# Spreading the weight conversions over all twelve attention tiles, with earlier loads and the conditional copies on another queue

## The chip, the cores and the metric

One core of a Trainium2 chip runs the whole kernel. The metric is the device time of one execution in microseconds. Several executions are compared by their median.

## The reference

Three layers run one after the other on a tensor of 2 batches, 768 positions and 384 = 8 x 48 features.

```python
# 1. linear attention with decay, per batch b and head h
cur = einsum('bhd,bhe->bhde', u * k_t, v_t)
y_t = einsum('bhd,bhde->bhe', r_t, state + cur)
state = w * state + einsum('bhd,bhe->bhde', k_t, v_t)
# 2. mixing over tokens, then over channels
h = relu(x.T @ w_tok1) @ w_tok2;  u = x + h.T
x = u + relu(u @ w_ch1) @ w_ch2
# 3. one expert per token (8 experts); the choice can be carried over from the token before
out = p[e] * (relu(x @ w1[e]) @ w2[e])
```

The weights of layer 2 (`w_tok1`, `w_tok2`, `w_ch1`, `w_ch2`) are 64-bit floats in memory. The kernel needs each of them as two 32-bit numbers, a high and a low part, so that three fast matmuls give a product of nearly full precision. Making these two parts is the conversion that this document is about.

## The kernel before

**Attention.** The 12 tiles (`NT`) are 128 positions each, six per batch. The loop `for t in range(NT)` works on several tiles at once: in pass t, TensorE makes the scores of tile t+1 and the values of tile t, VectorE multiplies r and k of tile t+2 with decay powers (`pre_rk`), masks the scores of t+1 (`masks`), forms a product of t+2 (`pre_beta`) and adds up x of tile t (`finish`). ScalarE copies `ks` (`pre_ks`), scales the state (`state`), makes the bonus of tile t+1 in eight small steps (`pre_bonus2`, written `bon`), and casts x to its high part `xh`; GpSimd subtracts to get the low part `xl`. Behind `finish`, `turn` transposes x of the tile before, `mix1` adds the first token matmul, and from tile 7 on `mix2` does a piece of the second one for batch 0; its VectorE step adds into `xT`. In tile 10 `usplit` splits the first part of `xT` (ScalarE `uh`, VectorE `ul`).

**Conversions.** There are 16 blocks (`conv`), two for each of eight weight tiles. Block n goes through these steps:

- a load of 768 KB into one of two `raw` buffers (`conv_load`, SyncE's queue);
- abs(n): ScalarE takes the magnitude of the upper words (`conv_abs`, L305);
- part A: two VectorE steps (L314, L315); part B: one (L319); part C: one (L321), after which the next raw block is loaded into the freed buffer. `conv_do(k)` runs the next k parts;
- hi(n) and lo(n): ScalarE casts the result to the high part (L281), GpSimd subtracts for the low part (L282). This is `conv_finish`, called at the beginning of the next part A or by itself.

Blocks 0 to 7 belong to the attention loop, blocks 8 and 9 to the stretch behind it (`conv_tail`), and blocks 10 to 15 to the first twelve channel steps (`later`). Before the change, `CONV_T` lists the eight tiles that hold a block: in each of them `conv_abs` stands ahead of `values`, parts A and B ahead of `finish`, part C behind it:

```python
        if t in CONV_T:
            conv_abs(CONV_T.index(t))
        values(t)
...
        if t in CONV_T:
            conv_do(CONV_N[t])
        else:
            conv_finish()
        finish(t)
        if t in CONV_T:
            conv_do(3 - CONV_N[t])
```

**What sets the order.** The order on each engine is the order in which the program is written; each engine takes its instructions strictly one after the other. PSUM tiles come from five buffers in turn, so the score tiles of a later pass wait until `finish` has read an earlier one. SyncE's queue issues all loads and, in `finish`, a copy from `yscr` into x (L477) that is carried out only if a decay lies outside the fast path's range (`bad > 0`); with these inputs it is not. Loads of `rk` have four buffers, those of `v` three.

Of the kernel before, what the change touches and what calls it, by code (L numbers as in the profile page):

```python
# [9 lines left out]
F32 = mybir.dt.float32  # L10
# [10 lines left out]
DM = H * D  # L21
NCH = S // 128
NT = B * NCH
# [5 lines left out]
W_LO, W_HI = 0.55, 1.25  # L29
WARM = (6, 12, 3)  # L30
T1 = 4
CONV_T = (2, 3, 4, 5, 6, 8, 9, 10)
CONV_B = (1, 1, 1, 1, 1, 1, 0, -1, 0, 0)
ABS_NEXT = (10, 11, 12, 13, 14)
ABS_B = (0, 3)
CONV_N = (0, 0, 2, 2, 2, 2, 2, 2, 2, 2, 2, 0)
HI_MIN, HI_MAX = (float(x) for x in np.array([0x38100000, 0x47EFFFFF], np.int32).view(np.float32))

CST = {}
# [38 lines left out]
def _emit(ctx, tc, a_in, wu, u_row, wt1, wt2, wc1, wc2, wgl, wex, cst_in, cst_a, out):  # L78
    nc = tc.nc
# [7 lines left out]
    yscr = dram.tile([NT, 128, DM], F32, name="yscr")  # L87
# [11 lines left out]
    def C(name):  # L99
        a, b = CST[name]  # L100
        return cst[:, a:b]
# [10 lines left out]
    ap = actx.enter_context(tc.tile_pool(name="ap", bufs=2))  # L112
# [21 lines left out]
    def load_a(t, part=None):  # L134
        if t not in a_t:
            rk = ap.tile([128, 1024], F32, tag="rk", name=f"rk{t}", bufs=4)
            v = ap.tile([128, DM], F32, tag="v", name=f"v{t}", bufs=3)
            a_t[t] = (rk, v)
        for p, (dst, c0) in enumerate(zip(a_t[t], (0, 1536))):
            if part is None or p == part:  # L140
                nc.sync.dma_start(out=dst, in_=a_in[t, :, c0:c0 + dst.shape[1]])
# [43 lines left out]
    for k in range(1, 7):  # L185
# [8 lines left out]
        if k == 5:  # L194
            bad = nc.values_load(bad_i[0:1, 0:1], min_val=0, max_val=1)
# [59 lines left out]
    conv = []  # L255
# [3 lines left out]
    conv_raw, conv_pend, cpool_, wb2 = [], [], [], []  # L259
    nload = [0]  # L260

    def conv_load():
        n = nload[0]
        if n >= len(conv) or (n >= 12 and not cpool_):
            return
        nload[0] += 1
        k, h = conv[n]
        src = wt1 if k == 0 else wt2 if k == 1 else None
        if src is None:
            src = (wc1, wc2)[k % 2][(k - 2) // 2]  # L270
        if n < 12:
            raw = rawp.tile([128, 768, 2], I32, tag="raw", name="raw")
        else:
            raw = cpool_[0].tile([128, 768, 2], I32, tag=f"e{n - 12}", name="raw")
        nc.sync.dma_start(out=raw.rearrange("p n t -> p (n t)"), in_=src.bitcast(I32)[:, h * 1536:(h + 1) * 1536])
        conv_raw.append(raw)

    def conv_finish():
        if conv_pend:
            f, hs, ls = conv_pend.pop()  # L280
            nc.scalar.copy(hs, f)  # L281
            nc.gpsimd.tensor_tensor(out=ls, in0=f, in1=hs.bitcast(F32), op=ALU.subtract)  # L282
# [4 lines left out]
    def conv_abs(n):  # L287
        k, h = conv[n]
        name = ("t1", "t2", "c10", "c20", "c11", "c21", "c12", "c22")[k]
        if h == 0:  # L290
            pool = wtp if k < 2 else wbl if k < 5 else wb2[0]
            W[name] = tuple(pool.tile([128, 1536], F32R, tag=f"b{2 * k + j}", name=name) for j in range(2))
        raw = conv_raw.pop(0)
        parts = tuple(x[:, h * 768:(h + 1) * 768] for x in W[name])
        if wb2:
            if n < 12:
                late[n % 2] = cpool_[0].tile([128, 1536], I32, tag=f"raw{6 + n % 2}", name="f")
            f, mag = late[n % 2][:, 0:768], late[n % 2][:, 768:1536].bitcast(F32)
        else:
            if n % 2:  # L300
                f = hp.tile([128, 768], I32, tag="row", name="f", bufs=1)
            else:
                f = ap.tile([128, 768], I32, tag="f", name="f", bufs=1)
            mag = f.bitcast(F32)
        nc.scalar.activation(out=mag, in_=raw[:, :, 1].bitcast(F32), func=ACTF.Abs)  # L305
        conv_mag[n] = raw, mag, f, parts

    def conv_parts():
        for n in range(len(conv)):
            conv_finish()  # L310
            if n not in conv_mag:
                conv_abs(n)
            raw, mag, f, parts = conv_mag.pop(n)
            nc.vector.tensor_scalar(out=mag, in0=mag, scalar1=HI_MIN, scalar2=HI_MAX, op0=ALU.max, op1=ALU.min)  # L314
            nc.vector.tensor_scalar(  # L315
                out=f, in0=mag.bitcast(I32), scalar1=3, scalar2=0x3FFFFFFF, op0=ALU.logical_shift_left, op1=ALU.bitwise_and
            )
            yield
            nc.vector.scalar_tensor_tensor(out=f, in0=raw[:, :, 0], scalar=29, in1=f, op0=ALU.logical_shift_right, op1=ALU.bitwise_or)  # L319
            yield  # L320
            nc.vector.scalar_tensor_tensor(out=f, in0=raw[:, :, 1], scalar=-0x40000000, in1=f, op0=ALU.bitwise_and, op1=ALU.bitwise_or)  # L321
            conv_pend.append((f.bitcast(F32), *parts))
            conv_load()
            if n in ABS_NEXT:
                conv_abs(n + 1)
            yield
        conv_finish()

    tail_at = [-1]

    def conv_tail(n):
        tail_at[0] += 1
        for j in range(2):
            if ABS_B[j] == tail_at[0]:
                conv_abs(8 + j)
        if n < 0:
            conv_finish()
        else:
            conv_do(n)

    conv_work = conv_parts()

    def conv_do(n=3):
        for _ in range(n):
            next(conv_work, None)
# [45 lines left out]
    def scores(t):  # L391
        rk = a_t[t][0]
        at_t[t] = [ps_tile("at0"), ps_tile("at1")]
        for q in range(4):
            for g in range(2):
                r0 = 64 * g
                nc.tensor.matmul(
                    at_t[t][g][:, q * 128:(q + 1) * 128],
                    lhsT=rk[r0:r0 + 64, 512 + q * 128:512 + (q + 1) * 128],
                    rhs=rk[r0:r0 + 64, q * 128:(q + 1) * 128],  # L400
                    start=True,
                    stop=True,
                )
# [29 lines left out]
    def old(t):  # L433
        kp = ps_tile("kp")
        kp_t[t] = kp[:, 0:384].rearrange("p (q e) -> p q e", q=4)
        beta_t[t] = kp[:, 384:392]
        if t % NCH in range(1, NCH - 1):
            nc.tensor.matmul(kp_t[t], lhsT=CA("ident"), rhs=sts[(t - 1) % 3], start=True, stop=False)
# [34 lines left out]
    def finish(t):  # L473
        b, c = divmod(t, NCH)
        x = ap.tile([128, DM], F32, tag="x", name="x")
        nc.vector.tensor_tensor(out=x, in0=y_t.pop(t), in1=bon_t.pop(t).rearrange("p h e -> p (h e)"), op=ALU.add)
        nc.sync.dma_start(out=x, in_=yscr[t], cond=bad > 0, cond_hint=False)  # L477
        xh[t] = ap.tile([128, DM], F32R, tag=f"xh{c}", name=f"xh{t}", bufs=1)
        xl[t] = ap.tile([128, DM], F32R, tag=f"xl{c}", name=f"xl{t}", bufs=1)
        nc.scalar.copy(xh[t], x)  # L480
        nc.gpsimd.tensor_tensor(out=xl[t], in0=x, in1=xh[t].bitcast(F32), op=ALU.subtract)
        xx[t] = x
# [79 lines left out]
    for t in range(NT):  # L562
        if t + 3 < NT:
            load_a(t + 3, 0)
        if t < 2:
            conv_load()
        grow = t + 1 < NT and (t + 1) % NCH < NCH - 1
        if t + 1 < NT:
            old(t + 1)
            scores(t + 1)  # L570
            if t == 0:
                warm_up(WARM[2])
        if t + 2 < NT:
            pre_rk(t + 2)
        if t + 1 < NT:
            masks(t + 1)
            beta(t + 1)
        if t + 2 < NT:
            pre_beta(t + 2)
        if grow:  # L580
            update(t + 1)
            state(t + 1)
        if t in CONV_T:
            conv_abs(CONV_T.index(t))
        values(t)
        if t + 1 < NT:
            pre_bonus2(t + 1)
        if t + 3 < NT:
            load_a(t + 3, 1)
        if t in CONV_T:  # L590
            conv_do(CONV_N[t])
        else:
            conv_finish()
        finish(t)
        if t in CONV_T:
            conv_do(3 - CONV_N[t])
        if t >= 7:
            mix2(*m2.pop(0))
        if t == 10:
            usplit(0)  # L600
        if t >= 1:
            turn(t - 1)
            m1.append(t - 1)
            if t >= T1:
                for _ in range(2):
                    if m1:
                        mix1(m1.pop(0))
        if t + 2 < NT and (t + 2) % NCH < NCH - 1:
            pre_ks(t + 2)
# [649 lines left out]
    with tc.If(nreg > 0):  # L1259
        with tc.tile_pool(name="ov", bufs=1) as ovp:  # L1260
# [9 lines left out]
                out=sel, in0=pfx.unsqueeze(1).to_broadcast([128, NOV, 96]), in1=C("ovn").unsqueeze(2).to_broadcast([128, NOV, 96]), op=ALU.is_equal  # L1270
# [91 lines left out]
```

## Time and profile before

| what | us |
|---|---|
| median of 3 runs | 428.48 (425.42 to 428.80) |
| the profiled execution | 426.03 |
| its span, first to last instruction | 424.5 |
| TensorE busy | 398.8 |
| VectorE busy | 278.4 |
| ScalarE busy | 193.0 |
| GpSimd busy | 90.3 |

A timeline row reads: start in us, duration in us, engine and line, operation, out<-in with the shape, the number of instructions merged into the row, and in brackets how long the engine was idle ahead of it and what released it. The start of a row and the start of the next one tell more than the durations, since one instruction's end overlaps the next one's start by about 0.1 us. DVE is VectorE, ACT is ScalarE, POOL is GpSimd, PE is TensorE and SPq the queue of SyncE.

### The profile page before, as it was taken

To read this page: it belongs to the slowest core of one execution; us is meant where nothing else is said; L and a number is where in the kernel's file an instruction comes from. 1 tells how busy PE (TensorE), PEld (TensorE's weight loads), DVE (VectorE), ACT (ScalarE), POOL (GpSimd) and SP (SyncE) were. 2 spreads that over 40 slices of the span, in tenths; PEclk is the share of its full clock that TensorE was granted. 3 is DMA by queue.
4 is the path that set the end of the run, shared out by engine and by line. 5 is a ranking of instruction groups with operands and counts; after the bars stand their busy time and mean duration, and the time that the engine had idled before them with its cause. 6 is when DMAs were issued, how large, how long until landed. Compare 5 with 4: busy or idle time off the path is not lost. (4 is left out here: it accounts for less than half of the span.)

```text
span 424.5 us, 8637 instructions
## 1 busy us (share of the span) xinstructions
PE 398.8 (94%) x3348; PEld 380.6 (90%) x3348; DVE 278.4 (66%) x592; ACT 193.0 (45%) x459; POOL 90.3 (21%) x83
## 2 busy tenths in 40 slices
PE   6898699997898899999999999999999999999994
PEld 3677688986797899999999999999999999999994
DVE  6869998986989833624361446659677676675431
ACT  1688386783343332112311221642755666654531
POOL 2004345054323310000000001131261132111110
PEclk9998999998999699999999999999999999999998
DMA  7455565333380000100100010881879866663000
GB/s 263 162 174 152 204 218 189 100 90 117 114 350 2 1 2 19 38 0 2 56 2 0 2 56 16 320 312 44 264 287 411 273 216 234 214 203 102 12 30 14
DMA packets 16800, 55.88 MB, mean 132 GB/s; under 512 B 3921, under 2 KB 7795, under 8 KB 16754
## 3 DMA queue, kind: packets, MB, share of 16 engines
q1 hardware_dynamic: 14834, 49.96, 33.7%
q0 software_dynamic: 1920, 5.32, 4.0%
q8 instruction: 27, 0.44, 0.4%
q14 instruction: 19, 0.16, 0.1%
HBM read 52.31 MB, written 5.91 MB: 137 GB/s over the span
## 5 line engine op out<-in xcount | busy, mean ns | idle before, releaser
L1024 DVE TENSOR_TENSOR we<-wr,we 128x768 fp32r<-128x768 f32 x54 | 51.6, 961 | 14.5 <-ACT we L1023 14.2
L353 ACT ACTIVATE hh<-c 128x384 fp32r<-128x384 f32 x48 | 23.5, 490 | 74.7 <-PE c L350 66.1
L354 DVE SCALAR_TENSOR_TENSOR hl<-c,hh 128x384 fp32r<-128x384 f32 x48 | 26.5, 552 | 43.8 <-ACT hh L353 43.8
L353 ACT ACTIVATE hh<-e 128x256 fp32r<-128x256 f32 (+1 forms) x72 | 25.2, 350 | 57.2 <-PE e L350 42.3
L348 PE MATMUL c<-uh,c 128*128 128x384 f32 x144 | 49.2, 342 | 2.1 <-ACT c L281 2.1
L354 DVE SCALAR_TENSOR_TENSOR hl<-e,hh 128x256 fp32r<-128x256 f32 (+1 forms) x72 | 27.2, 378 | 35.2 <-ACT hh L353 35.1
L348 PE MATMUL acc<-hh,c 128*128 128x384 f32 x144 | 50.2, 349 | 0.0
L349 PE MATMUL c<-uh,c 128*128 128x384 f32 x144 | 49.0, 340 | 1.2 <-POOL c L282 1.2
L349 PE MATMUL acc<-hh,c 128*128 128x384 f32 x144 | 48.8, 339 | 0.0
L350 PE MATMUL acc<-hl,c 128*128 128x384 f32 x144 | 48.8, 339 | 0.0
L350 PE MATMUL c<-ul,c 128*128 128x384 f32 x144 | 48.8, 339 | 0.0
L1023 ACT CAST we<-wr 128x768 fp32r<-128x768 f32 x56 | 46.1, 830 | 3.1 <-DMA wr<-in_wex 3.1
L348 PE MATMUL acc<-we,hh 128*128 128x384 f32 x120 | 42.6, 355 | 0.0
L349 PE MATMUL acc<-we,hl 128*128 128x384 f32 x120 | 40.3, 336 | 0.0
L350 PE MATMUL acc<-we,hh 128*128 128x384 f32 x120 | 40.2, 335 | 0.0
L282 POOL TENSOR_TENSOR c<-f,c 128x768 fp32r<-128x768 f32 x12 | 24.3, 2026 | 45.1 <-ACT c L281 45.1
L348 PEld LDWEIGHTS c<-uh,c 128*128 128x128 f32 x144 | 27.7, 192 | 2.4 <-ACT c L281 2.4
L349 PEld LDWEIGHTS c<-uh,c 128*128 128x128 f32 x144 | 27.6, 192 | 1.8 <-POOL c L282 1.8
L349 PEld LDWEIGHTS acc<-hh,c 128*128 128x128 f32 x144 | 27.5, 191 | 0.0
L348 PEld LDWEIGHTS acc<-hh,c 128*128 128x128 f32 x144 | 27.5, 191 | 0.0
L350 PEld LDWEIGHTS acc<-hl,c 128*128 128x128 f32 x144 | 27.5, 191 | 0.0
L350 PEld LDWEIGHTS c<-ul,c 128*128 128x128 f32 x144 | 27.4, 191 | 0.0
(228 smaller groups left out, 945.0 us busy)
## 6 DMA issues: line engine op xcount, KB each, us to landing
wr<-in_wex SPq DMA_DIRECT2D x32, 768.0 KB
raw<-in_wc SPq DMA_DIRECT2D x12, 768.0 KB
rk<-in_a_in SPq DMA_DIRECT2D x12, 512.0 KB
raw<-in_wt SPq DMA_DIRECT2D x4, 768.0 KB
v<-in_a_in SPq DMA_DIRECT2D x12, 192.0 KB
x<-yscr SPq DMA_DIRECT2D x12, 192.0 KB
xs<-rows SPq DMA_DIRECT2D x8, 192.0 KB
xs<-row SPq DMA_DIRECT2D x4, 192.0 KB
```

The costliest lines, as they stand in the source:

```text
L282: nc.gpsimd.tensor_tensor(out=ls, in0=f, in1=hs.bitcast(F32), op=ALU.subtract)
L348: nc.tensor.matmul(ps, lhsT=lh, rhs=rh, start=first, stop=False)
L349: nc.tensor.matmul(ps, lhsT=ll, rhs=rh, start=False, stop=False)
L350: nc.tensor.matmul(ps, lhsT=lh, rhs=rl, start=False, stop=last)
L353: nc.scalar.activation(out=hi, in_=ps, func=ACTF.Relu)
L354: nc.vector.scalar_tensor_tensor(out=lo, in0=ps, scalar=0.0, in1=hi.bitcast(F32), op0=ALU.max, op1=ALU.subtract)
L1023: nc.scalar.copy(hi[:, cs], raw[:, cs])
L1024: eng.tensor_tensor(out=lo[:, cs], in0=raw[:, cs], in1=hi[:, cs].bitcast(F32), op=ALU.subtract)
```

## The change

- The parts of blocks 0 to 7 are spread over all tiles: two parts in each of tiles 0 to 9, three in tile 10, all ahead of `finish`, and the last one behind `finish` of tile 11. The sequence by tiles is A0 B0, C0 A1, B1 C1, A2 B2, C2 A3, B3 C3, A4 B4, C4 A5, B5 C5, A6 B6, C6 A7 B7, C7.
- abs(n+1) is issued right after part C of block n, at the place of that part in the pass, and abs(0) right ahead of part A of block 0. These places are behind `pre_bonus2`.
- Both raw buffers are asked for in tile 0; `v` gets a fourth buffer.
- The conditional copy is issued by ScalarE.
- In `conv_tail` abs(8) and abs(9) follow C7 and C8.

```diff
--- before.py
+++ after.py
@@ -29,11 +29,8 @@
 W_LO, W_HI = 0.55, 1.25
 WARM = (6, 12, 3)
 T1 = 4
-CONV_T = (2, 3, 4, 5, 6, 8, 9, 10)
+CONV_N = (2, 2, 2, 2, 2, 2, 2, 2, 2, 2, 3, 1)
 CONV_B = (1, 1, 1, 1, 1, 1, 0, -1, 0, 0)
-ABS_NEXT = (10, 11, 12, 13, 14)
-ABS_B = (0, 3)
-CONV_N = (0, 0, 2, 2, 2, 2, 2, 2, 2, 2, 2, 0)
 HI_MIN, HI_MAX = (float(x) for x in np.array([0x38100000, 0x47EFFFFF], np.int32).view(np.float32))
 
 CST = {}
@@ -134,7 +131,7 @@
     def load_a(t, part=None):
         if t not in a_t:
             rk = ap.tile([128, 1024], F32, tag="rk", name=f"rk{t}", bufs=4)
-            v = ap.tile([128, DM], F32, tag="v", name=f"v{t}", bufs=3)
+            v = ap.tile([128, DM], F32, tag="v", name=f"v{t}", bufs=4)
             a_t[t] = (rk, v)
         for p, (dst, c0) in enumerate(zip(a_t[t], (0, 1536))):
             if part is None or p == part:
@@ -321,18 +318,12 @@
             nc.vector.scalar_tensor_tensor(out=f, in0=raw[:, :, 1], scalar=-0x40000000, in1=f, op0=ALU.bitwise_and, op1=ALU.bitwise_or)
             conv_pend.append((f.bitcast(F32), *parts))
             conv_load()
-            if n in ABS_NEXT:
+            if n + 1 < len(conv) and (n + 1 < 10 or wb2) and conv_raw:
                 conv_abs(n + 1)
             yield
         conv_finish()
 
-    tail_at = [-1]
-
     def conv_tail(n):
-        tail_at[0] += 1
-        for j in range(2):
-            if ABS_B[j] == tail_at[0]:
-                conv_abs(8 + j)
         if n < 0:
             conv_finish()
         else:
@@ -474,7 +465,7 @@
         b, c = divmod(t, NCH)
         x = ap.tile([128, DM], F32, tag="x", name="x")
         nc.vector.tensor_tensor(out=x, in0=y_t.pop(t), in1=bon_t.pop(t).rearrange("p h e -> p (h e)"), op=ALU.add)
-        nc.sync.dma_start(out=x, in_=yscr[t], cond=bad > 0, cond_hint=False)
+        nc.scalar.dma_start(out=x, in_=yscr[t], cond=bad > 0, cond_hint=False)
         xh[t] = ap.tile([128, DM], F32R, tag=f"xh{c}", name=f"xh{t}", bufs=1)
         xl[t] = ap.tile([128, DM], F32R, tag=f"xl{c}", name=f"xl{t}", bufs=1)
         nc.scalar.copy(xh[t], x)
@@ -562,7 +553,8 @@
     for t in range(NT):
         if t + 3 < NT:
             load_a(t + 3, 0)
-        if t < 2:
+        if t == 0:
+            conv_load()
             conv_load()
         grow = t + 1 < NT and (t + 1) % NCH < NCH - 1
         if t + 1 < NT:
@@ -580,20 +572,16 @@
         if grow:
             update(t + 1)
             state(t + 1)
-        if t in CONV_T:
-            conv_abs(CONV_T.index(t))
         values(t)
         if t + 1 < NT:
             pre_bonus2(t + 1)
         if t + 3 < NT:
             load_a(t + 3, 1)
-        if t in CONV_T:
+        if t < NT - 1:
             conv_do(CONV_N[t])
-        else:
-            conv_finish()
         finish(t)
-        if t in CONV_T:
-            conv_do(3 - CONV_N[t])
+        if t == NT - 1:
+            conv_do(CONV_N[t])
         if t >= 7:
             mix2(*m2.pop(0))
         if t == 10:
```

On ScalarE in tiles 0 and 1, before (`st` is the state, `xh` the cast of x, `f<-raw` the abs of a block):

```order
L382 COPY beta<-kp 128x8
L385 ACTIVATE bon<-v_106,beta 128x48 x8
L480 CAST xh_422<-x 128x384
L376 COPY ks<-kt 128x512
L467 ACTIVATE st_188<-kp,w_184 128x96 x4
L382 COPY beta<-kp 128x8
L385 ACTIVATE bon<-v_294,beta 128x48 x8
L480 CAST xh_517<-x 128x384
```

and after the change:

```order
L373 COPY beta<-kp 128x8
L376 ACTIVATE bon<-v_106,beta 128x48 x8
L302 ACTIVATE f<-raw 128x768
L468 ISA
L468 DMA x<-yscr 128x384
L471 CAST xh_431<-x 128x384
L367 COPY ks<-kt 128x512
L458 ACTIVATE st_188<-kp,w_184 128x96 x4
L373 COPY beta<-kp 128x8
L376 ACTIVATE bon<-v_294,beta 128x48 x8
L302 ACTIVATE f<-raw 128x768
L278 CAST t_421<-f 128x768
```

The abs of blocks 0 and 1, the cast of hi(0) (`t<-f`) and the conditional copy with its register step (ISA) stand between the bonus steps and the cast of x.

On VectorE from the masks of tile 10 (`am`) to the addition into `xT` behind tile 11, before:

```order
L409 TENSOR_TENSOR am_1454<-at_1444,cst 128x512
L409 TENSOR_TENSOR am_1456<-at_1445,cst 128x512
L314 TENSOR_SCALAR f<-f 128x768
L315 TENSOR_SCALAR f<-f 128x768
L319 SCALAR_TENSOR_TENSOR f<-raw,f 128x768
L476 TENSOR_TENSOR x<-y,bon 128x384
L321 SCALAR_TENSOR_TENSOR f<-raw,f 128x768
L523 TENSOR_TENSOR xT_521<-xT_521,acc_1519 128x384
L534 TENSOR_TENSOR ul<-xT_521,uh 128x384 x3
L476 TENSOR_TENSOR x<-y,bon 128x384
L523 TENSOR_TENSOR xT_521<-xT_521,acc_1584 128x384
```

and after the change:

```order
L400 TENSOR_TENSOR am_1451<-at_1441,cst 128x512
L400 TENSOR_TENSOR am_1453<-at_1442,cst 128x512
L318 SCALAR_TENSOR_TENSOR f<-raw,f 128x768
L311 TENSOR_SCALAR f<-f 128x768
L312 TENSOR_SCALAR f<-f 128x768
L316 SCALAR_TENSOR_TENSOR f<-raw,f 128x768
L467 TENSOR_TENSOR x<-y,bon 128x384
L514 TENSOR_TENSOR xT_537<-xT_537,acc_1516 128x384
L525 TENSOR_TENSOR ul<-xT_537,uh 128x384 x3
L467 TENSOR_TENSOR x<-y,bon 128x384
L318 SCALAR_TENSOR_TENSOR f<-raw,f 128x768
L514 TENSOR_TENSOR xT_537<-xT_537,acc_1586 128x384
```

C6 now stands ahead of A7 (L311, L312) and B7 (L316) in tile 10, and C7 (L318) has moved from behind the first x to behind the second.

In SyncE's queue around the load of rk for tile 10 (`rk_1093` before, `rk_1090` after), before:

```order
L477 ISA
L477 DMA x<-yscr 128x384
L275 DMA raw<-in_wc 128x1536
L141 DMA rk_971<-in_a_in 128x1024
L141 DMA v_972<-in_a_in 128x384
L477 ISA
L477 DMA x<-yscr 128x384
L275 DMA raw<-in_wc 128x1536
L141 DMA rk_1093<-in_a_in 128x1024
L141 DMA v_1094<-in_a_in 128x384
```

and after the change:

```order
L138 DMA rk_860<-in_a_in 128x1024
L138 DMA v_861<-in_a_in 128x384
L272 DMA raw<-in_wc 128x1536
L138 DMA rk_975<-in_a_in 128x1024
L138 DMA v_976<-in_a_in 128x384
L138 DMA rk_1090<-in_a_in 128x1024
L138 DMA v_1091<-in_a_in 128x384
L272 DMA raw<-in_wc 128x1536
```

The conditional copies are gone from this queue, and the raw block that stood right ahead of that load is now ahead of the load for tile 9.

## Rows read from the trace of the kernel before

**Rows 1.** Table by stage: us; busy time (x) of PE, PEld, DVE, ACT, POOL; clock, DMA.

```profile
28.00:70.00 42.00, 34.95 (x541) 30.76 (x537) 40.97 (x50) 28.76 (x90) 16.34 (x9) 0.96 0.51 167
70.00:92.00 22.00, 22.00 (x338) 19.73 (x335) 18.73 (x28) 15.75 (x50) 7.16 (x5) 1.00 0.44 142
...
118.00:150.00 32.00, 28.68 (x149) 27.73 (x148) 29.91 (x33) 12.54 (x19) 11.27 (x6) 0.89 0.26 103
```

**Rows 2.** Timeline of VectorE, tiles 0 to 2: start, us, line, work [idle before].

```profile
16.19 0.68 DVE L368 TENSOR_TENSOR pp<-rk 128x512 f32<-128x512 f32 x1
17.67 0.56 DVE L476 TENSOR_TENSOR x<-y,bon 128x384 f32<-128x384 f32 x1 [0.80 <-PE y L427]
...
23.08 0.56 DVE L476 TENSOR_TENSOR x<-y,bon 128x384 f32<-128x384 f32 x1 [1.28 <-PE y L427]
...
25.65 1.29 DVE L409 TENSOR_TENSOR am<-at,cst 128x512 f32<-128x512 f32 x2 [0.88 <-PE at L397]
...
28.61 0.56 DVE L314 TENSOR_SCALAR f<-f 128x768 f32<-128x768 f32 x1 [1.07 <-ACT f L305]
...
29.80 0.96 DVE L319 SCALAR_TENSOR_TENSOR f<-raw,f 128x768 int32<-128x768 int32 x1
30.67 0.55 DVE L476 TENSOR_TENSOR x<-y,bon 128x384 f32<-128x384 f32 x1
31.14 0.95 DVE L321 SCALAR_TENSOR_TENSOR f<-raw,f 128x768 int32<-128x768 int32 x1
```

**Rows 3.** Timeline of ScalarE, tiles 0 to 2.

```profile
17.85 1.91 ACT L385 ACTIVATE bon<-v,beta 128x48 f32<-128x48 f32 x8
19.67 0.50 ACT L480 CAST xh<-x 128x384 fp32r<-128x384 f32 x1
...
22.60 1.91 ACT L385 ACTIVATE bon<-v,beta 128x48 f32<-128x48 f32 x8
...
27.64 0.93 ACT L305 ACTIVATE f<-raw 128x768 f32<-128x768 f32 x1
...
31.34 0.51 ACT L480 CAST xh<-x 128x384 fp32r<-128x384 f32 x1 [0.77 <-DMA x<-yscr]
```

**Rows 4.** Timeline of SyncE's queue, tiles 0, 2 and 7.

```profile
6.84 0.51 SPq L275 DMA_DIRECT2D raw<-in_wt  x1
...
31.25 0.09 SPq L477 DMA_DIRECT2D x<-yscr  x1
...
66.37 0.33 SPq L275 DMA_DIRECT2D raw<-in_wc  x1
66.75 1.02 SPq L141 DMA_DIRECT2D rk<-in_a_in  x1
```

**Rows 5.** Timeline of VectorE, tiles 3 to 11, and later.

```profile
38.27 2.57 DVE L321 SCALAR_TENSOR_TENSOR f<-raw,f 128x768 int32<-128x768 int32 x1
...
43.91 2.29 DVE L368 TENSOR_TENSOR pp<-rk 128x512 f32<-128x512 f32 x1
...
73.02 1.81 DVE L363 TENSOR_TENSOR rk<-rk,PP 128x1024 f32<-128x1024 f32 x1 [1.92 <-DMA rk<-in_a_in]
...
90.08 0.56 DVE L314 TENSOR_SCALAR f<-f 128x768 f32<-128x768 f32 x1 [1.01 <-ACT f L305]
...
93.94 5.12 DVE L534 TENSOR_TENSOR ul<-xT,uh 128x384 fp32r<-128x384 f32 x3
...
99.45 0.54 DVE L523 TENSOR_TENSOR xT<-xT,acc 128x384 f32<-128x384 f32 x1
...
151.41 1.60 DVE L534 TENSOR_TENSOR ul<-xT,uh 128x384 fp32r<-128x384 f32 x3 [1.31 <-ACT uh L533]
```

**Rows 6.** Timeline of GpSimd, tile 3.

```profile
38.19 1.83 POOL L282 TENSOR_TENSOR t<-f,t 128x768 fp32r<-128x768 f32 x1 [5.25 <-ACT t L281]
```

**Rows 7.** Timeline of TensorE behind the last tile.

```profile
100.04 0.48 PE L348 MATMUL acc<-t,t1h 128*128 128x384 f32 x1 [2.46 <-DVE xT L523]
```

**Rows 8.** DMA issues of the whole run: work, engine, count, median us to landing.

```profile
out<-rows,si POOLq DMA_INDIRECT x9, 2.5
```

## The prediction

> **What bounds the kernel now.** I read the stage table first, then the order of work on VectorE, then ScalarE, then the transfers. A tile of the attention loop is one pass of `t`; x(t) is its last VectorE step, A, B and C are the three conversion parts of a block, and abs(n), hi(n), lo(n) are the block's steps on ScalarE (two) and GpSimd. In the stage table [rows 1] the reader is to see three regimes: from 28 to 70 us VectorE is busy 40.97 of 42 us and TensorE is not full; from 70 to 92 us TensorE is busy all 22.00 us; from 118 to 150 us VectorE is again the full one (29.91 of 32), with the conversions of blocks 10 to 15. Behind that TensorE runs without a gap that this change touches. So the change acts on the time at which the attention loop ends, and I carry a shift there one to one to the end: the stages behind are the same instructions in the same order.
>
> In tiles 0 to 2 VectorE stands idle [rows 2]: 0.80 and 1.28 us before x(0) and x(1), 0.88 before the masks, and 1.07 before the first conversion, 4.03 in all. These rows also give the durations. From x(1) at 23.08 to the masks at 25.65, less 0.88, is 1.69; from there to A0 at 28.61, less 1.07, is 1.89: a tile without conversions costs VectorE 3.58. A is 1.19 (28.61 to 29.80), B 0.87 (to 30.67), x 0.47 (to 31.14), and C I take like B at 0.87: a block is 2.93.
>
> **Tiles 0 to 3: the four parts moved forward, +1.8 us.** The change puts A0 and B0 in tile 0, C0 and A1 in tile 1. Their work, 1.19 + 0.87 + 0.87 + 1.19 = 4.1, would just fill the idle 4.03. But abs(0) used to be ahead of the eight bonus steps in ScalarE's order, and now it is behind them. The eight take 1.91 from 17.85, and the next step began at 19.67 [rows 3]; with the 0.93 of an abs [rows 3], A0 starts at 20.6 and x(0), 2.06 later, at 22.7, where it was 17.67: 5.0 late. The cover of 0.80 is used up, and VectorE stands from 16.87 (end of 16.19 + 0.68) to 20.6.
>
> What is queued behind x(0) on ScalarE is xh(0), ks(2), the state, and the eight bonus steps of tile 1. From xh at 19.67 to those eight at 22.60 were 2.9 us [rows 3]. With xh(0) at about 23.45 they start at 26.4, and abs(1) ends behind them at 26.4 + 1.8 + 0.9 = 29.1. VectorE has x(0), the multiply, the masks, the product (3.58) and C0 (0.87) done at 22.7 + 4.45 = 27.1, so A1 waits 2 us. x(1) is then at 29.1 + 1.2 = 30.3, against 23.08. In tile 2 the earlier 0.88 and 1.07 are gone, but lo(0) on GpSimd now meets the next multiply (below); I put 1.3 there. x(2): 30.3 + 3.58 + 1.3 + 1.74 = 36.9. x(3): 36.9 + 3.58 + 2.06 = 42.5, with 8 parts done. Before, x(3) ended at 38.27 [rows 5], so it began at 37.8, with 5 parts done; with three more it would be 40.7. So +1.8. The bounds: -2.7 if no wait arises (4.03 filled, less the 1.3), +3.0 if the new idle of 3.7 and 2.0 and the 1.3 stand against the 4.03 alone. I take what the walk through the queues gives.
>
> The blocks themselves come in time. The first raw block is asked for at 6.84 [rows 4] as before, the second and v(3) now right behind it; v gets a fourth buffer, so its load no longer holds SyncE until v(0) is free. I cost these at nothing: what hides them is the 12.8 us from 6.84 to abs(0) at 19.67. Were that cover too short, A0 would wait for the block, and tile 0 would end later by as much.
>
> **Tiles 4 to 6: -2.7 us.** Before, lo(0) on GpSimd, 1.83 us from 38.19 [rows 6], stood beside C1, which took 2.57 instead of 0.95; lo(1) did the same to a product, 2.29 instead of 0.68 [rows 5]. A third such block falls in these tiles, so 3 x 1.6 = 4.8. In the new order lo(1) comes while the masks run, whose input is in PSUM (0.1 by my walk), and lo(2) meets a multiply, 1.3: a gain of 3.4. Against it, in tile 4 C2 is followed at once by A3, whose abs(3) is behind the bonus steps: a wait of 0.7. Bounds: lo(1) and lo(2) may each cost 1.8 (then -0.5 in place of -2.7), or nothing (-4.1).
>
> The Trainium skill has a rule for this: "SBUF — State Buffer", section "Who interferes with whom": a VectorE instruction with two SBUF inputs and a GpSimd instruction that reads SBUF share a port pair, and the one issued second is blocked in full. This case's 2.57 beside 1.83 agrees. By that rule each lo costs up to its whole 1.83 or nothing, by where it falls; the sum would be by it 3.4 worse if lo(0), lo(1), lo(2) and lo(6) all fell on such work.
>
> **Tiles 7 to 9: -0.3 us.** VectorE loses one part per tile here in comparison, and the 1.92 us for which it waited for the rk block [rows 5] should go: that load was issued at 66.75 right behind a raw block at 66.37 [rows 4], and in the new order no raw load stands between the two rk loads. But TensorE was busy without a gap [rows 1], and its work is unchanged, so most of this is hidden anyway. It equally hides the wait for abs(5), about 1, in tile 7 and one for t1h, which C3 used to cover. I take -0.3, bounds -1.9 and +1.9.
>
> **Tiles 10 and 11: 0.** Before: 1.01 of idle ahead of A7 and 5.12 for three ul steps that alone take 1.60 [rows 5]; 1.01 + 3.52 = 4.5. After: abs(7) is behind the bonus steps and nothing covers it, because this tile has neither multiply nor product: wait 2.1; lo(6) meets B7, 1.1; C6 comes in, 0.87; the ul steps meet only one short GpSimd step, 0.5: 4.6. C7 goes behind x(11), but still ahead of the xT addition at 99.45 that releases TensorE, which had waited 2.46 for it [rows 7]; lo(7) goes behind that, where VectorE has slack.
>
> **The conditional copies.** Twelve are taken from SyncE's queue and put on ScalarE's, each with its register step. On SyncE one took 0.09, from 31.25, and xh ran at 31.34 [rows 3, 4]: an untaken copy releases its reader at once. I take 0 for the move (a hand-over less, a register step more). Queued behind each on ScalarE are xh, xT and ks, and the whole of the next tile. The bounds are 0 and, from the nearest row for a transfer that must land, 2.5 [rows 8]. SyncE, which no longer waits for x, issues rk earlier; that is late nowhere else.
>
> **Sum.** +1.8 - 2.7 - 0.3 + 0 = -1.2 us on the profiled execution's 426.03 (span 424.5 and 1.53 around it): 424.8. That execution is 2.45 under the median of the three runs, 428.48; on the median it is 427.3, which I forecast: no change that can be told (a measurement of this kernel tells about 1%, 4.3 us, from none).
>
> **Rivals.** (a) The parts fill the idle time as meant: no wait for abs(0) and abs(1), so tiles 0 to 3 give -2.7 in place of +1.8, in all -5.7, 422.8. For it: 4.03 of idle against 4.1 of work, and no row shows the new queue order. Against it: ScalarE runs in order, and the eight bonus steps end at 19.76. Chance 0.22.
> (b) Slower: the copy on ScalarE's queue isn't over at once but costs up to 2.5. Its place is the loop x(t), copy, xh, ks, state, bonus, abs, A, which closes where A follows C: tiles 1, 7 and 10. Price 3 x 2.4 = 7.2, in all +6.0, 434.5. It turns the sum over from 0.4 us per copy and passes 1% from 1.8. Against it: 0.09 on SyncE. Chance 0.14.
> (c) The lo steps fall on two-input work throughout: lo(0) +0.5, lo(1) +1.7, lo(2) +0.5, lo(6) +0.7, in all +2.2, 430.7. For it: both rows of before that stand in rows 5 show it; against: the masks are a third of a tile. Chance 0.15.
>
> **How the numbers follow.** My forecast has 0.49. Its own range is 425 to 430. Faster by over 1%: (a) and a little of the forecast, 0.25. Slower: (b) and some of (c), 0.20. Within 1%: 0.55. The range leaves out the far half of (a) and most of (b): 421.5 to 433.
>
> **What would show it.** Right: VectorE idle before the first conversion from about 17 to 20.6, x(0) near 22.7, x(1) near 30; a wait of about 2 before A1 and before A7 on ScalarE's abs; x(3) near 42.5; the last xT addition of the loop near 98; the rk wait of 1.92 gone. Wrong: x(1) before 28 speaks for (a); xh more than 1 us behind the end of x on an idle ScalarE for (b); conversions of 2.4 us and more in tiles 4 to 6 for (c). If the loop ends 3 us earlier or later and the time doesn't follow, the one-to-one carry is wrong.

## The result, and the profile after

| | median us | range |
|---|---|---|
| before, 22 runs | 427.71 | 424.93 to 431.61 |
| after, 22 runs | 429.74 | 427.87 to 435.19 |
| ratio after to before | 1.0054 | 95% interval 1.0029 to 1.0079 |

The ratios and intervals, here and below, leave out runs more than 1.5% above the fastest of their kernel (two of the 22 of after, five of the twelve of `e1_copies`), while medians and ranges hold all runs. The change costs 2.0 us. That is within 1%, as was the likeliest of the three cases, but it lies on the other side of the forecast of -1.2, and the interval excludes the forecast. That 429.74 lies inside the prediction's own range of 425 to 430 does not show that its steps hold; they are taken one by one below. The profiled executions are 426.03 (span 424.5) before and 431.61 (span 430.1) after: 1.7 under and 1.9 over their medians, so a difference of spans overstates the change.

The starts of x(t) show where the time comes from. The steps are those of the prediction; x(3) of before, 37.80 with 5 parts done, is set three parts (2.93) later to compare equal work.

| mark | before | after | forecast of the step | measured |
|---|---|---|---|---|
| x(3), 8 parts done | 40.73 | 42.46 | +1.8 | +1.7 |
| x(6), 14 parts done | 63.43 | 65.65 | -2.7 | +0.5 |
| x(9), 20 parts done | 86.00 | 88.56 | -0.3 | +0.3 |
| last xT addition of the loop | 99.45 | 103.16 | 0 | +1.1 |
| ul steps behind 150 us | 151.41 | 154.87 | carried 1:1 | +3.5 in all |

The same stage table as in [rows 1], of the kernel after, with a window in tile 5 added: us; busy time (x) of PE, PEld, DVE, ACT, POOL; clock, DMA.

```profile
28.00:70.00 42.00, 38.50 (x601) 34.17 (x598) 34.86 (x47) 28.52 (x89) 16.54 (x10) 0.92 0.51 180
70.00:92.00 22.00, 21.30 (x333) 19.05 (x331) 18.57 (x28) 15.64 (x52) 8.04 (x5) 1.00 0.33 106
118.00:150.00 32.00, 28.44 (x149) 27.62 (x149) 27.93 (x32) 12.10 (x18) 11.42 (x6) 0.92 0.36 130
51.00:59.00 8.00, 7.30 (x77) 7.04 (x78) 7.04 (x11) 3.68 (x12) 2.97 (x2) 0.57 0.50 169
```

The same added window of the kernel before:

```profile
51.00:59.00 8.00, 7.66 (x126) 6.86 (x125) 7.86 (x12) 4.18 (x13) 3.49 (x3) 1.00 0.59 200
```

From 28 to 70 us VectorE was the full engine, 40.97 of 42; now it is busy 34.86, and TensorE 38.50 at a granted clock of 0.92. From 70 to 92 us and from 118 to 150 us little has changed. The clock of 51 to 59 us says why TensorE takes longer: 0.57, where before it was 1.00.

VectorE after, answering to [rows 2] and [rows 5] (start, us, line, work, idle before and its releaser):

```profile
20.58 0.56 DVE L311 TENSOR_SCALAR f<-f 128x768 f32<-128x768 f32 x1 [3.71 <-ACT f L302]
...
22.65 0.55 DVE L467 TENSOR_TENSOR x<-y,bon 128x384 f32<-128x384 f32 x1
...
29.52 0.56 DVE L311 TENSOR_SCALAR f<-f 128x768 f32<-128x768 f32 x1 [2.52 <-ACT f L302]
...
30.59 0.55 DVE L467 TENSOR_TENSOR x<-y,bon 128x384 f32<-128x384 f32 x1
31.06 2.37 DVE L354 TENSOR_TENSOR rk<-rk,PP 128x1024 f32<-128x1024 f32 x1
...
42.46 0.55 DVE L467 TENSOR_TENSOR x<-y,bon 128x384 f32<-128x384 f32 x1
...
45.28 1.12 DVE L359 TENSOR_TENSOR pp<-rk 128x512 f32<-128x512 f32 x1
46.32 1.78 DVE L318 SCALAR_TENSOR_TENSOR f<-raw,f 128x768 int32<-128x768 int32 x1
...
49.54 2.40 DVE L354 TENSOR_TENSOR rk<-rk,PP 128x1024 f32<-128x1024 f32 x1
...
56.47 0.55 DVE L467 TENSOR_TENSOR x<-y,bon 128x384 f32<-128x384 f32 x1
...
61.78 1.29 DVE L400 TENSOR_TENSOR am<-at,cst 128x512 f32<-128x512 f32 x2 [3.63 <-PE at L388]
...
65.65 0.55 DVE L467 TENSOR_TENSOR x<-y,bon 128x384 f32<-128x384 f32 x1
...
91.08 1.29 DVE L400 TENSOR_TENSOR am<-at,cst 128x512 f32<-128x512 f32 x2 [1.50 <-PE at L388]
...
94.58 0.56 DVE L311 TENSOR_SCALAR f<-f 128x768 f32<-128x768 f32 x1 [1.35 <-ACT f L302]
...
95.78 2.49 DVE L316 SCALAR_TENSOR_TENSOR f<-raw,f 128x768 int32<-128x768 int32 x1
...
99.86 2.05 DVE L525 TENSOR_TENSOR ul<-xT,uh 128x384 fp32r<-128x384 f32 x3 [0.66 <-ACT uh L524]
...
103.16 0.54 DVE L514 TENSOR_TENSOR xT<-xT,acc 128x384 f32<-128x384 f32 x1
...
154.87 1.60 DVE L525 TENSOR_TENSOR ul<-xT,uh 128x384 fp32r<-128x384 f32 x3 [0.80 <-ACT uh L524]
```

In tile 0 VectorE now stands for 3.71 us and in tile 1 for 2.52, both for ScalarE's abs. The masks at 61.78 wait 3.63 for TensorE. In tile 10 there are waits of 1.50 and 1.35, and B7 takes 2.49. The ul steps, 5.12 in [rows 5], are 2.05. No wait for an rk block is left (1.92 in [rows 5]).

ScalarE after, answering to [rows 3]:

```profile
17.84 1.91 ACT L376 ACTIVATE bon<-v,beta 128x48 f32<-128x48 f32 x8
19.66 0.89 ACT L302 ACTIVATE f<-raw 128x768 f32<-128x768 f32 x1
23.23 0.13 ACTq L468 DMA_DIRECT2D x<-yscr  x1
23.40 0.51 ACT L471 CAST xh<-x 128x384 fp32r<-128x384 f32 x1 [2.85 <-DMA x<-yscr]
...
26.78 1.91 ACT L376 ACTIVATE bon<-v,beta 128x48 f32<-128x48 f32 x8
28.60 0.89 ACT L302 ACTIVATE f<-raw 128x768 f32<-128x768 f32 x1
```

Abs(0) starts at 19.66, where xh(0) stood in [rows 3], behind the eight bonus steps; abs(1) at 28.60, behind the next eight. The conditional copy takes 0.13, and xh runs right behind it.

SyncE's queue after, answering to [rows 4]: the load of rk for tile 10, with no raw block right in front of it.

```profile
59.31 0.42 SPq L138 DMA_DIRECT2D rk<-in_a_in  x1
```

GpSimd after, answering to [rows 6]: lo(0), lo(2) and lo(6) stand beside the rk multiplies at 31.06 and 49.54 and beside B7 at 95.78.

```profile
30.29 2.06 POOL L279 TENSOR_TENSOR t<-f,t 128x768 fp32r<-128x768 f32 x1 [5.09 <-ACT t L278]
...
49.04 1.82 POOL L279 TENSOR_TENSOR t<-f,t 128x768 fp32r<-128x768 f32 x1 [1.76 <-ACT t L278]
...
95.35 2.10 POOL L279 TENSOR_TENSOR c<-f,c 128x768 fp32r<-128x768 f32 x1 [2.93 <-ACT c L278]
```

TensorE after, in tile 5 and (last row) behind the last tile, answering to [rows 7]:

```profile
49.68 0.63 PE L437 MATMUL kp<-uw,pp 128*64 128x2 f32 x16 [0.40 <-DVE x L467]
51.22 0.89 PE L446 MATMUL kp<-v,ks 128*64 128x48 f32 x16 [0.91 <-ACT ks L367]
52.59 1.55 PE L413 MATMUL y<-st,rk 128*64 128x96 f32 x16 [0.48 <-DVE am L400]
...
57.73 0.52 PE L340 MATMUL acc<-xh,t 128*128 128x384 f32 x1
...
58.54 0.34 PE L340 MATMUL acc<-xh,t 128*128 128x384 f32 x1
...
103.76 0.44 PE L339 MATMUL acc<-t,t1h 128*128 128x384 f32 x1 [1.82 <-DVE xT L514]
```

It waited 0.40, 0.91 and 0.48 between 49 and 53 us and was busy 0.91 of the 2 us from 49 to 51; its granted clock was at the lower level, 1.2 GHz, from 51.5 to 58.3, so the first two of these waits lie ahead of the fall and the third behind it. The rows at 57.73 and 58.54 are the same step of `mix1` at the two levels, 0.52 and 0.34. Behind the last tile its wait for the xT addition is 1.82 where [rows 7] has 2.46.

### The profile page after: what moved, and what is told of

It is laid out like the page before. It is cut to its first block, busy times and chain, and to the rows that moved or that the text cites. A ratio compares the mean times of both kernels' runs of the same rounds, so it can differ in the third digit from the quotient of the medians.

```text
span 430.1 us, 8633 instructions
## 1 busy us (share of the span) xinstructions
PE 402.2 (94%) x3348; PEld 383.3 (89%) x3348; DVE 274.3 (64%) x592; ACT 192.4 (45%) x459; POOL 89.2 (21%) x83
## 5 line engine op out<-in xcount | busy, mean ns | idle before, releaser
L339 PE MATMUL c<-uh,c 128*128 128x384 f32 x144 | 48.3, 336 | 2.1 <-ACT c L278 2.1
L340 PE MATMUL c<-uh,c 128*128 128x384 f32 x144 | 48.6, 337 | 1.5 <-POOL c L279 1.5
L279 POOL TENSOR_TENSOR c<-f,c 128x768 fp32r<-128x768 f32 x12 | 23.0, 1917 | 46.1 <-ACT c L278 41.3
L339 PEld LDWEIGHTS c<-uh,c 128*128 128x128 f32 x144 | 27.0, 188 | 2.4 <-ACT c L278 2.4
L340 PEld LDWEIGHTS c<-uh,c 128*128 128x128 f32 x144 | 27.1, 188 | 1.9 <-POOL c L279 1.9
L339 PE MATMUL e<-gx,we 128*128 128x256 f32 x96 | 27.3, 284 | 0.0
```

Source lines behind the costliest of these rows:

```text
L339: nc.tensor.matmul(ps, lhsT=lh, rhs=rh, start=first, stop=False)
L340: nc.tensor.matmul(ps, lhsT=ll, rhs=rh, start=False, stop=False)
```

## The experiments

Four readings were put against each other first. P: the new places of the parts cost the time; Q: the copies on ScalarE's queue do. Within P, P1: it is the waits for abs behind the bonus steps; P2: it is TensorE's clock in tile 5. All ratios are to the kernel before, with 95% intervals.

**Places without copies and buffers (`e1_sched`).** After, with two lines as before:

```diff
-            v = ap.tile([128, DM], F32, tag="v", name=f"v{t}", bufs=4)
+            v = ap.tile([128, DM], F32, tag="v", name=f"v{t}", bufs=3)
-        nc.scalar.dma_start(out=x, in_=yscr[t], cond=bad > 0, cond_hint=False)
+        nc.sync.dma_start(out=x, in_=yscr[t], cond=bad > 0, cond_hint=False)
```

> The changed kernel with its copies back on SyncE's queue and three v buffers: the new places of the parts alone. Theory P (the places of the parts cost the time, through the waits for abs in tiles 0, 1 and 10 and through TensorE at its lower clock in tile 5): as slow as the changed kernel, ratio 1.003 to 1.008, x(0) again at 22.6. Theory Q (the conditional copies on ScalarE cost it): like before, 0.997 to 1.002, xh less than 0.15 us behind the copy in both.

Measured: 429.94, ratio 1.0067 (1.0038 to 1.0096). x(0) starts at 22.64, x(3) at 42.39, the last xT addition at 102.06. The whole loss is there without the copies: P. TensorE's clock from 51 to 59 us was 0.79 in this execution, the masks of tile 7 waited 2.54 for it, and x(5) to x(6) took 8.09 us (56.41 to 64.50), where after has 0.57, 3.63 and 9.18.

**Copies alone (`e1_copies`).** Before, with the copy issued by `nc.scalar`.

> The kernel before with nothing but the twelve conditional copies on ScalarE. Theory P: no change, ratio 0.998 to 1.002, the copy itself 0.09 to 0.13 us. Theory Q: 1.004 to 1.008, with xh later behind the end of x.

Measured: 428.9, ratio 0.9979 (0.9943 to 1.0016): no difference by the runs that the ratio keeps; the median of all twelve lies 0.3% above that of before, which is still under what Q asked for. Its ScalarE, in tile 2:

```profile
33.25 0.09 ACTq L477 DMA_DIRECT2D x<-yscr  x1
33.38 0.51 ACT L480 CAST xh<-x 128x384 fp32r<-128x384 f32 x1 [0.81 <-DMA x<-yscr]
```

The copy takes 0.09, and xh starts 0.13 behind the copy's start, where it was 0.09 on SyncE's queue [rows 3, 4]. Q falls, by `e1_sched` above all.

**Abs ahead of the bonus in every tile (`e1_abs`).** After, with every abs of the loop ahead of `values`, as in the kernel before:

```diff
+ABS_T = (0, 1, 3, 4, 6, 7, 9, 10)
-            if n + 1 < len(conv) and (n + 1 < 10 or wb2) and conv_raw:
+            if n + 1 >= 8 and n + 1 < len(conv) and (n + 1 < 10 or wb2) and conv_raw:
                 conv_abs(n + 1)
...
+        if t in ABS_T:
+            conv_abs(ABS_T.index(t))
         values(t)
```

> The changed kernel with abs(n) ahead of the bonus steps in each tile that holds part A of block n. Theory P1 (the waits for abs are what costs): x(0) at about 20.7 and x(1) at about 26 instead of 22.65 and 30.59, the wait of 2.5 before A1 and of 1.35 before A7 gone, loop end 2 to 4 us earlier, ratio to before 0.994 to 1.000. Theory P2 (TensorE's clock falling in tile 5 costs it, 3 us): whatever is gained in tiles 0 and 1 is lost again by tile 6 if the clock falls there, ratio 1.002 to 1.007; if the clock happens not to fall, as P1.

Measured: 424.4, ratio 0.9943 (0.9915 to 0.9970): faster than before, and by the two ratios 1.1% faster than after. On VectorE:

```profile
18.58 0.56 DVE L312 TENSOR_SCALAR f<-f 128x768 f32<-128x768 f32 x1 [1.71 <-ACT f L303]
...
20.65 0.55 DVE L468 TENSOR_TENSOR x<-y,bon 128x384 f32<-128x384 f32 x1
...
37.77 0.56 DVE L312 TENSOR_SCALAR f<-f 128x768 f32<-128x768 f32 x1 [1.27 <-ACT f L303]
...
39.83 0.55 DVE L468 TENSOR_TENSOR x<-y,bon 128x384 f32<-128x384 f32 x1
```

x(0) comes 2.0 us earlier than after (22.65), x(3) 2.6. The wait of A1 is gone, as expected, but A0 and A2 still wait, 1.71 and 1.27. TensorE was busy 8.00 of 8 us from 51 to 59 here, at 1.00, so this run holds P1 and P2 together.

**The first two alone (`e2_abs01`) and the last alone (`e2_abs10`).** As above, with `ABS_AT = {0: 0, 1: 1}` or `{10: 7}` (pass: block) in place of `ABS_T`; all other abs stay behind part C.

> The changed kernel with only abs(0) and abs(1) ahead of the bonus steps of tiles 0 and 1. Theory P1 (waits in tiles 0 and 1 are the larger part): x(3) near 39.8 instead of 42.46, loop end 2 to 3 us earlier than in the changed kernel, ratio to before 0.996 to 1.001. Theory P2 (the clock and tile 10 are the larger part): x(3) earlier too, but the loop end less than 1.5 us earlier, ratio 1.001 to 1.005.

> The changed kernel with only abs(7) ahead of the bonus steps of tile 10. Theory P1: the wait of 1.35 before A7 goes and B7, no longer beside the GpSimd subtraction, is back at 0.96; loop end 1 to 3 us earlier, ratio to before 0.999 to 1.003. Theory P2: the same or less, as TensorE is late for the scores of tile 11 anyway: 1.003 to 1.006.

Measured: 426.32, 0.9952 (0.9914 to 0.9989), and 426.83, 0.9969 (0.9935 to 1.0004). Both medians are lower than theory P1 expected of one placement. Both profiled executions came 1 to 2 us later through their first tile than the others, with a granted clock of 0.77 and 0.89 between 8 us and x(0) where after has 1.00, so only stretches are compared. With the first two moved, A0 waits 1.71 and not 3.71, and x(0) to x(3) takes 17.82 (22.68 to 40.50) and not 19.81; the clock still fell in tile 5. With the last moved, VectorE in tile 10:

```profile
89.75 0.55 DVE L468 TENSOR_TENSOR x<-y,bon 128x384 f32<-128x384 f32 x1
...
94.35 0.55 DVE L312 TENSOR_SCALAR f<-f 128x768 f32<-128x768 f32 x1
...
95.53 0.96 DVE L317 SCALAR_TENSOR_TENSOR f<-raw,f 128x768 int32<-128x768 int32 x1
...
101.71 0.54 DVE L515 TENSOR_TENSOR xT<-xT,acc 128x384 f32<-128x384 f32 x1
```

The wait for abs(7), 1.35, is gone, and B7 is 0.96 again and not 2.49. From x(9) to the last xT addition are 11.96 us (89.75 to 101.71) where after has 14.60: 2.6 us from one instruction's place.

**Work for TensorE in tile 5 (`e1_fill`).** After, with nine matmuls into an accumulator that nothing reads, 2, 5 and 2 at three places of pass 5, so that TensorE waits less:

```diff
+FILL = {5: (2, 5, 2)}
+            nc.tensor.matmul(fp, lhsT=warm[:, 0:128], rhs=warm[:, 0:384], start=True, stop=True)
...
+            fill(FILL.get(t, (0, 0, 0))[0])
             beta(t + 1)
...
+        fill(FILL.get(t, (0, 0, 0))[1])
         if grow:
...
+        fill(FILL.get(t, (0, 0, 0))[2])
         values(t)
```

> The changed kernel with nine added 128x384 bf16 matmuls in tile 5, put where TensorE waits (2 before beta, 5 before the update, 2 before the values); they add nothing to any output. Theory P2: the granted clock stays at 1.00 from 51 to 59, the wait of 3.63 before the masks of tile 7 falls under 1, loop end 2.5 to 3 us earlier, ratio to before 0.997 to 1.001. Theory P1: the wait shrinks but the loop ends less than 1 us earlier, ratio 1.003 to 1.008, because VectorE is late anyway.

Measured: 428.15, ratio 1.0023 (0.9998 to 1.0048). The window of tile 5, then VectorE:

```profile
51.00:59.00 8.00, 7.71 (x105) 6.37 (x103) 7.07 (x11) 4.16 (x13) 2.98 (x2) 1.00 0.49 165
```

```profile
56.50 0.55 DVE L475 TENSOR_TENSOR x<-y,bon 128x384 f32<-128x384 f32 x1
...
59.19 1.29 DVE L408 TENSOR_TENSOR am<-at,cst 128x512 f32<-128x512 f32 x2 [1.01 <-PE at L396]
...
63.06 0.55 DVE L475 TENSOR_TENSOR x<-y,bon 128x384 f32<-128x384 f32 x1
```

The clock stays at 1.00, the masks wait 1.01 and not 3.63, and x(6) starts at 63.06 and not at 65.65: nine matmuls more made the tile 2.6 us shorter. x(5) starts at 56.50 in it and 56.47 after, so nothing ahead differs. With `e1_sched` between them, x(5) to x(6) goes 9.18, 8.09, 6.56 as the clock of that window goes 0.57, 0.79, 1.00. P2 holds in the trace. In the medians the gain is 1.6 us; the ratio lies between the ranges of P1 and P2, and its interval overlaps that of after, so the medians don't show it.

**The same idea on the kernel before (`e2_bfill`).** Six such matmuls ahead of `values` in pass 2, `FILL = {2: (0, 0, 6)}`.

> The kernel before with six added bf16 matmuls in tile 2, ahead of the values, where TensorE waits before its clock falls at 35.7; they add nothing to any output. Theory P2 with its condition (a lower clock costs only where TensorE bounds; tile 3 of the kernel before is VectorE's): the clock stays up there or not, and the ratio is 0.997 to 1.003. Rival (a lower clock costs wherever it is): 0.993 to 0.997.

Measured: 427.56, ratio 0.9986 (0.9948 to 1.0023). The clock of 35 to 40 us was 0.66, as it was before without them, so this run does not tell what a held clock would give there: inconclusive. Its trace shows something else: the clock fell in tile 5 too, under the old places of the parts. The stretch from x(4) to x(5), first of the kernel before, then of this run:

```profile
48.18:55.45 7.27, 5.37 (x95) 5.11 (x96) 7.12 (x13) 4.27 (x13) 2.06 (x1) 1.00 0.62 210
49.25:56.52 7.27, 5.37 (x86) 5.07 (x87) 7.13 (x13) 4.26 (x13) 2.06 (x1) 0.77 0.52 182
```

**Abs where ScalarE waits (`e2_start`, `e3_start_again`).** After, with the five abs that a part A follows closely at the very start of the pass, where ScalarE waits for the state; the other three stay behind part C:

```diff
+ABS_AT = {0: 0, 1: 1, 4: 3, 7: 5, 10: 7}
-            if n + 1 < len(conv) and (n + 1 < 10 or wb2) and conv_raw:
+            if n + 1 not in ABS_AT.values() and n + 1 < len(conv) and (n + 1 < 10 or wb2) and conv_raw:
                 conv_abs(n + 1)
...
             conv_load()
+        if t in ABS_AT:
+            conv_abs(ABS_AT[t])
         grow = t + 1 < NT and (t + 1) % NCH < NCH - 1
```

> The changed kernel with abs(0), abs(1), abs(3), abs(5) and abs(7) at the very start of tiles 0, 1, 4, 7 and 10, where ScalarE waits for TensorE, and abs(2), abs(4), abs(6) still behind part C of the tile before. Theory P1: no wait before any part A, x(0) near 19, x(3) near 38.5, loop end 1 to 3 us earlier than with all abs just ahead of the bonus steps, ratio to before 0.986 to 0.993. Rival (TensorE bounds tiles 5 to 10, so that VectorE's earlier arrival there is worth nothing): 0.993 to 0.997.

> The kernel with abs at the start of the tiles, once more beside the two above, for a ratio on the same chip. Theory P: 0.975 to 0.985, loop end near 92. Rival (the first look was a lucky one): 0.985 to 0.993.

Measured: 419.27, ratio 0.9794 (0.9740 to 0.9848), and with the same code again 418.27, 0.9786 (0.9742 to 0.9829): 2.1% faster than before, and more than either theory expected. The second run's window, ScalarE and VectorE:

```profile
28.00:70.00 42.00, 39.25 (x669) 34.97 (x665) 39.09 (x54) 32.36 (x105) 17.88 (x11) 1.00 0.54 188
```

```profile
15.87 0.94 ACT L303 ACTIVATE f<-raw 128x768 f32<-128x768 f32 x1 [0.23 <-DMA raw<-in_wt]
```

```profile
18.91 0.55 DVE L468 TENSOR_TENSOR x<-y,bon 128x384 f32<-128x384 f32 x1
...
36.23 0.55 DVE L468 TENSOR_TENSOR x<-y,bon 128x384 f32<-128x384 f32 x1
...
90.64 0.54 DVE L515 TENSOR_TENSOR xT<-xT,acc 128x384 f32<-128x384 f32 x1
```

Abs(0) starts at 15.87 and not at 19.66, A0 waits for nothing, x(0) comes at 18.91, x(3) at 36.23 (42.46 after), the last xT addition at 90.64 (103.16). From 28 to 70 us the granted clock is 1.00, so this run, like `e1_abs`, holds the gain from the waits and that from the clock together.

**Its copies and buffers taken back (`e3_startsp`).** The same with the two lines of `e1_sched`.

> The kernel with abs at the start of tiles 0, 1, 4, 7 and 10, but with the conditional copies back on SyncE and three v buffers. Theory P (places alone): as fast as with them, ratio to before 0.977 to 0.985. Theory R (once the waits are gone, SyncE's queue held up by the copies becomes the next limit): 0.985 to 0.995, with a wait for a block of rk or v on VectorE or ScalarE.

Measured: 418.63, ratio 0.9800 (0.9758 to 0.9841), the same time. By these runs the copies and the fourth v buffer neither give nor cost anything.

**Early abs on the kernel before (`e3_bstart`).** Before, with `conv_abs` moved from ahead of `values` to the start of the pass.

> The kernel before, its parts where they were, with abs at the start of each tile that holds a block instead of ahead of the values. Theory S (the even spread pays once no part A waits for its abs; the place of abs alone does nothing here, as only two waits of 1.0 stand in its trace): ratio 0.996 to 1.001. Rival (the early abs itself is the gain): 0.980 to 0.990.

Measured: 424.69, ratio 0.9918 (0.9885 to 0.9951), the expected 1 is missed. Of the waits of 1.07 in [rows 2] and 1.01 in [rows 5] the first is gone and 0.34 is left of the second; x(2) starts at 29.50, where it was 30.67. So of the 2.1%, the place of the abs alone gives 0.8, and the rest needs the even spread as well.

## Why the prediction was wrong

- **Tiles 0 to 3, +1.8: right.** Measured +1.7, by the walk's own steps: A0 at 20.58 (20.6), x(0) 22.65 (22.7), A1 after a wait of 2.52 (2.0), x(1) 30.59 (30.3), lo(0) beside the multiply 2.37 - 1.22 = 1.15 more (1.3), x(2) 37.00 (36.9), x(3) 42.46 (42.5). `e1_abs`, `e2_abs01` and `e2_start` show the cause: with the abs earlier these waits shrink or go.
- **Tiles 4 to 6, -2.7: this step failed**, +0.5. Its terms for VectorE were near in sum: lo(1) cost 1.12 - 0.68 on a product, lo(2) 2.40 - 1.22 on a multiply, and GpSimd's xl (45.81 to 47.28), which the step lacked, 1.78 - 0.95 on C2; that is 2.45, with no wait of A3, against 0.1 + 1.3 + 0.7. What the step did not hold is TensorE. It was costed as an engine with room [rows 1], at the full clock; but its clock was at 1.2 GHz for most of tile 5, and the masks then waited 3.63 for scores. With the clock up (`e1_fill`) x(6) lies 0.4 ahead of before, which makes the step -2.1. So 2.6 of the miss of 3.2 is the clock, between these two profiled executions. The trace of before, from which the step was costed, was a favourable one in this: in two others with the old places of the parts the clock from x(4) to x(5) was 0.61 (`e3_bstart`) and 0.77 (`e2_bfill`), and x(5) to x(6) took 8.74 and 9.05 us, where before has 1.00 and 7.98. So the clock falls in tile 5 without the change too, and how much of the 2.0 us between the medians it makes is not shown.
- **Tiles 7 to 9, -0.3: near,** +0.3. The rk wait went, and TensorE hid it, as argued.
- **Tiles 10 and 11, 0: mis-sized by 1.1.** From x(9) to the end both kernels do the same four parts; the 0.87 counted for C6 was in before as well, so the step's own sum should have been -0.8. Waits and stretched steps before were 4.53; after they are 1.35 (A7, put at 2.1), 2.49 - 0.96 (B7, put at 1.1), 2.05 - 1.60 (ul, 0.5), and two that the step lacked: 1.50 for TensorE's scores and 0.66 for uh. That is 5.49, 1.0 more. The rule of the Trainium skill in "SBUF — State Buffer", "Who interferes with whom", is that VectorE work with two SBUF inputs and GpSimd's reads of SBUF exclude each other. The runs agree: B7, with two SBUF inputs, grew by 1.53 beside lo(6) of 2.10, and by nothing in `e2_abs10`, where B7 starts at 95.53 and lo(6) at 96.42.
- **Copies, 0: right,** by `e1_copies` and `e3_startsp`.
- **Carry to the end: right as far as 151 us,** +3.7 at the loop's end and +3.5 there. Behind it the two profiled spans part by another 2.1 us, and this is not the change's: from these ul steps to the end eleven of the thirteen traces take 273.0 to 273.4 us, `e1_sched` and `e1_fill` among them, and only after and `e3_bstart` take 275.2 and 275.1. In these two one ScalarE step of layer 3 (hh, at 318.59 in after) waits 4.15 and 4.16 us, where none of the others has such a wait of more than 2.5 between 300 and 330 us; what held it stays open.
- **Rivals.** (a) falls with x(1) at 30.59; the idle time is filled as meant only where the abs is placed apart, and then it is worth more than (a) said, 418 to 419 us. (b) falls: xh starts 0.17 behind the copy's start in tile 0 of after, and `e1_sched` is slow without the copies. (c) was half right: lo(0), lo(2) and lo(6) did meet two-input work, lo(1) in part.

So the loss has one cause that both the traces and the medians show: ScalarE's order in tiles 0, 1 and 10. Moving the abs of tiles 0 and 1 alone takes the ratio from 1.0054 to 0.9952, that of tile 10 alone to 0.9969, and neither interval reaches that of after (1.0029 to 1.0079). TensorE's clock in tile 5 costs 2.6 us in the profiled execution of after, but its share in the medians is open. That the clock falls because of the waits just ahead is suggested by `e1_fill` alone; in `e1_abs` and `e2_start` it stayed up as well, but there the whole tile had changed.

## What to carry to other kernels

When work is moved in an engine's program, follow what it stands behind on every engine that feeds it: a 0.9 us step put behind 1.9 us of other steps let VectorE stand for 3.7 us in the first tile, and with five such steps put where their engine waits anyway +0.5% became -2.1%. Where one engine's load is thinned out, look at which becomes the bound, and if it is TensorE, cost it at both clock levels that the trace shows; one trace in which the clock happened to stay up is not enough. Time the parts of a change apart: here the spread was good and one placement hid it.

## What was not expected of the hardware

- A granted clock that was full at 45 us fell in tile 5 behind waits of 0.40 and 0.91 us, and cost 2.6 us there. Before, it fell in tile 3 (0.66 from 35 to 40 us), where VectorE was the bound. Whether it falls in tile 5 differs between executions of nearly the same program.
- The start of a program is not fixed: two runs of the same code (`e2_start`, `e3_start_again`) have x(0) at 20.89 and 18.91, which is as much as the whole effect of the change. From 8 to 17 us their granted clock was 0.62 and 1.00, and in other late starts (`e2_bfill`, `e2_abs01`, `e2_abs10`) it was 0.81, 0.62 and 0.81.
- An untaken copy between two steps of one engine costs 0.09 to 0.13 us on ScalarE's queue.
